# 168 keys of a block as 104 and 64 with the 64s of two heads transposed as one, v laid out by the host, key counts spread by a product, and a new order

## Chip, cores and metric

The kernel runs on one core of one Trainium2 chip. The metric is the device time of one execution in microseconds (us), a median over runs. The profile is of one execution; times inside it count from its first instruction.

## What is computed

Local attention with a few shared keys (4 batches, 8 heads of 64, 768 tokens), then a gated MLP with a product over the tokens:

```python
keep = (pos[None, :] < n_global) | ((rel >= 0) & (rel < n_local))      # 8 shared keys, 96 local ones
scores = where(keep, q @ k.T / 8 - slope[h] * dist, -1e9)
x = softmax(scores) @ v                                               # heads side by side: 4 x 768 x 512
h = relu(x @ w_in)                                                    # 512 -> 1024, halves u and v
v_s = einsum('ts,bsd->btd', w_spatial, layer_norm(v)) + b_spatial
out = (u * v_s) @ w_out                                               # 512 -> 512
```

## The kernel before

A block `n` is 128 queries of one batch (6 a batch, 24 in all; `i = n % 6`). A block with `i > 0` sees 168 keys: 64 queries need 8 shared and 96 local keys before their end, so each half of the block has its own 168. `prep` loads q and k. `scores` makes four score groups (16 small products on a quarter of the array each), then for each head one VectorE instruction (scale, bias, row minimum into `pr`) and one ScalarE exponential with its row sum. `values` transposes the probabilities on TensorE into PSUM tiles `p`, copies them to `pth` tiles, and multiplies them with `v`, two heads side by side in the array (64 columns each): the value product. Before, it cuts 168 keys into two chunks of 84 (`CK = KW // 2`): two transposes a head, 16 a block; a pair of heads fills one PSUM tile (84x512), so four copies a block (lines 830 to 839). Blocks with `i = 0` see 128 keys: 8 transposes and four copies of 128x256.

`prep_v` (line 742) loads v into one of two places of `vring`: for `i > 0` four pieces, of 84 and 76 rows for either half, and some of 8 rows for the shared keys; for `i = 0` one of 128 rows. All loads and stores are issued by SyncE's queue (SP), in order.

The MLP stages are called V (v half of `x @ w_in`, then the norm), U (u half), G (product with `w_spatial`), O (product with `w_out`). All inputs are float32, and the MLP weights are split into a high and a low float32r part by VectorE, ScalarE and GpSimd at the start (`split_weights`: tiles `u` and `wos` are loaded, `wc` is worked on, `w_in_h`, `w_in_l` and so on are the results; 8 tiles of w_in, of which V needs four and U the other four). The first batch's attention runs in the same stretch: below, the startup.

All instructions are recorded and then put in order by `plan` (line 339): a list scheduler over five engines, with a cost for each operation (`cost`) and a rank for each stage from the table `KEYS`; operations with several possible engines go where the plan starts them earliest. `keep_warm` (line 451) puts transposes of the identity (`s<-ident`, `m<-ident`, `p<-ident`: fillers, whose results nobody reads) into TensorE's long planned gaps.

The key counts `n_global` and `n_local` are loaded to all 128 partitions (lines 562, 563), made floats, and set the bias tiles, which the first softmax needs.

Of the kernel before, what the change touches and what calls it, by code (L numbers as in the profile page):

```python
# [26 lines left out]
CFG = {'vrelu': 'a', 'urelu': 'x', 'rs': 'p', 'bias0': 'xx', 'zero': 'pp', 'kept': 'pavp', 'bias1': 'vx', 'bias2': 'a', 'S': [['I01', 'A'], ['I00', 'T00', 'T01', 'A', 'V00', 'B00'], ['T02', 'T03', 'A', 'V01', 'U00'], ['T04', 'T05', 'A', 'V02'], ['Q00', 'Q01', 'A', 'V03', 'U01'], ['Q02', 'Q03', 'A', 'V04']], 'T': [['V15', 'U12', 'A'], ['G10', 'O10', 'A'], ['G11', 'O11', 'A'], ['G12', 'O12', 'V00', 'V01', 'U00', 'A'], ['V02', 'A'], ['V03', 'U01', 'A', 'V04']], 'END': ['V05', 'U02', 'G00', 'O00', 'G01', 'O01', 'G02', 'O02'], 'wcl': 'x', 'whi': 'x', 'wsub': 'x', 'wth': 'px', 'wtl': 'p', 'vhi': 'a', 'vlo': 'pp', 'qhi': 'x', 'qlo': 'x', 'khi': 'x', 'klo': 'x', 'pth0': 'aa', 'x0h': 'a', 'x0l': 'v', 'pth': 'x', 'xh': 'avva', 'c1': 'a', 'xl': 'pxxv', 'vnh': 'xapa', 'vnl': 'pvpv', 'gm': 'x', 'gh': 'aa', 'gl': 'x', 'o': 'vaaa', 'norm0': 'x', 'norm': 'x', 'vrn': 'v', 'fold': '0', 'div': 'x', 'rows': 'x', 'xf0h': 'x', 'xf0l': 'x', 'xbh': 'x', 'xbl': 'ppvv', 'b_rawqk': 1, 'b_ev': 3, 'b_raw': 1, 'b_pr': 10, 'b_pth': 5, 'b_c1': 2}  # L27
# [4 lines left out]
CK = KW // 2  # L32
# [184 lines left out]
def cost(op):  # L217
# [45 lines left out]
    return (180 if parts < P else 66) + (1.04 if parts < P else 1.1) * n, 0, not one  # L263


def shape_of(op):

    if op.eng != "tensor":
        return 0, 0
    if op.call != "together":  # L270
        return 0, 149 if op.call == "transpose" else 197
    return (1, 197) if list(op.args[0][2]["lhsT"].ap)[0][1] <= HALF else (2, 143)
# [66 lines left out]
def plan(ops, keys, trace=None):  # L339
# [18 lines left out]
    port, dma, mode = 0.0, 2500.0, 0  # L358
# [9 lines left out]
    while done < n:  # L368
# [115 lines left out]
WORDS = {"ev": 512, "gh": 1024, "gl": 1024, "pth": 512, "vring": 4096, "q": 512, "k": 960, "wos": 1024, "wts": 1536, "pr": 168, "s": 512, "p": 512, "m": 512, "c1": 512}  # L484
# [645 lines left out]
```

## Time and profile before

| | |
|---|---|
| median of 3 runs | 463.09 us (462.37 to 463.38) |
| the profiled execution | 462.34 us, its span 460.5 us |
| TensorE (PE) busy | 443.8 us, 96% of the span |
| VectorE (DVE), ScalarE (ACT), GpSimd (POOL) busy | 269.0, 196.6, 90.0 us |
| moved by DMA | 47.69 MB |

Busy times of PE are unions of overlapping matmuls, so the cost of one more matmul is read from the distance of starts or from the pieces of the chain of waits, not from its duration. A float32 product shows as two matmul records, a transpose as one.

### The profile page before, as it was taken

How to read it: one execution, taken by the hardware profiler on the slowest of the kernel's cores; microseconds unless marked ns; L12 is line 12 of the kernel's file. 1: busy time of each engine (PE TensorE's matmuls, PEld its weight loads, DVE VectorE, ACT ScalarE, POOL GpSimd, SP SyncE). 2: the span in 40 equal slices, each digit the busy share in tenths (PEclk: the TensorE clock that was granted, in tenths of full speed). 3: DMA queues.
4: the chain of work that ended last, by engine and by line, in shares of the span. 5: the costliest groups of instructions: out<-in, count | busy, mean ns of one | idle time of the engine just before them, and what ended most of it. 6: DMA issues, size and time to landing. Idle time of an engine off the chain costs nothing.

```text
span 460.5 us, 11598 instructions
## 1 busy us (share of the span) xinstructions
PE 443.8 (96%) x4621; PEld 398.5 (87%) x4621; DVE 269.0 (58%) x949; ACT 196.6 (43%) x594; POOL 90.0 (20%) x130
## 2 busy tenths in 40 slices
PE   6788999999999999999999999999999999999994
PEld 6577778899989989889989988989999888999994
DVE  5698988878883234686864334866632573324322
ACT  3558786657761121653762112666221362221111
POOL 2023456444120004221010003402100012330000
PEclk9899999999999999999999999999999999999998
DMA  6898775435641110334362110333111120000111
GB/s 187 254 308 254 222 249 159 124 125 168 203 142 74 47 47 0 111 97 125 106 210 95 47 46 1 127 124 98 41 47 47 45 60 1 1 2 2 46 47 53
DMA packets 23598, 47.69 MB, mean 104 GB/s; under 512 B 2704, under 2 KB 5008, under 8 KB 23536
## 3 DMA queue, kind: packets, MB, share of 16 engines
q1 hardware_dynamic: 23536, 46.87, 32.3%
q8 instruction: 38, 0.62, 0.6%
q14 instruction: 24, 0.20, 0.2%
HBM read 40.57 MB, written 6.29 MB: 102 GB/s over the span
## 4 chain that ended last, share of the span: by engine, by line
PE 86%; DVE 6%; DMA 3%; ACT 3%; issue 1%; SPq 0%; DVEq 0%
PE m L44 64%; PE p L44 17%; PE s L44 5%; DVE wc L44 2%; DMA u<-in_moe_w_in_dram 2%; DMA k<-in_k_dram 1%; ACT pr L44 1%; DVE pr L44 1%; DVE c L44 1%; DVE w_in_l L44 1%; SPq L44 0%; ACT w_in_h L44 0%; DVE pth L44 0%; ACT raw L44 0%; DVE xtl L44 0%
## 5 line engine op out<-in xcount | busy, mean ns | idle before, releaser
L44 ACT ACTIVATE pr<-pr,mn 128x168 f32<-128x168 f32 (+1 forms) x192 | 80.2, 419 | 18.7 <-DVE mn L44 16.5
L44 DVE CUSTOM_DVE_ANT_0 pr<-s,bias 128x168 f32<-128x168 f32 (+1 forms) x192 | 54.7, 316 | 22.7 <-PE p L44 15.9
L44 PE MATMUL p<-ident,pr 128*84 128x128 f32 (+1 forms) x352 | 54.6, 277 | 1.9 <-DVE c L44 0.6
L44 ACT ACTIVATE gh<-ev 128x512 fp32r<-128x512 f32 x24 | 15.1, 631 | 86.9 <-DVE ev L44 86.9
L44 DVE TENSOR_TENSOR ev<-m,b_bc 128x512 f32<-128x512 f32 x24 | 16.6, 690 | 60.7 <-PE m L44 60.6
L44 PEld LDWEIGHTS p<-pth,vring 84*64 84x64 f32 (+1 forms) x1344 | 43.2, 139 | 7.9 <-issue 3.3
L44 PE MATMUL p<-pth,vring 84*64 84x64 f32 (+1 forms) x1344 | 47.2, 228 | 2.7 <-ACT wc L44 2.6
L44 ACT ACTIVATE pth<-p 84x512 f32<-84x512 f32 (+1 forms) x65 | 35.8, 560 | 30.6 <-PE p L44 28.4
L44 ACT ACTIVATE ev<-m 128x512 f32<-128x512 f32 (+1 forms) x36 | 21.2, 590 | 64.4 <-PE m L44 64.4
L44 PEld LDWEIGHTS p<-ident,pr 128*84 128x84 f32 (+1 forms) x352 | 37.7, 122 | 11.0 <-ACT pr L44 1.9
L44 POOL TENSOR_TENSOR rs<-mv,eps 128x1 f32<-128x1 f32 x24 | 4.8, 201 | 197.6 <-DVE mv L44 123.3
L44 PE MATMUL m<-w_t_l,vnh 128*128 128x256 f32 x288 | 43.0, 283 | 0.0
L44 PE MATMUL m<-w_t_h,vnh 128*128 128x256 f32 x288 | 42.4, 282 | 0.0
L44 PE MATMUL m<-w_t_h,vnl 128*128 128x256 f32 x288 | 41.9, 281 | 0.0
L44 PEld LDWEIGHTS m<-w_t_h,vnh 128*128 128x128 f32 x288 | 37.9, 188 | 0.8
L44 PEld LDWEIGHTS m<-w_t_l,vnh 128*128 128x128 f32 x288 | 37.5, 188 | 0.0
L44 POOL TENSOR_TENSOR vnl<-ev,vnh 128x512 fp32r<-128x512 f32 x24 | 31.8, 1327 | 28.8 <-DVE vnh L44 21.5
L44 PEld LDWEIGHTS m<-w_t_h,vnl 128*128 128x128 f32 x288 | 37.2, 188 | 0.0
L44 ACT ACTIVATION_READ_ACCUMULATOR pr<-pr,mn 128x1 f32 x192 | 36.2, 188 | 0.0
L44 DVE TENSOR_SCALAR pr<-pr,rc 128x168 f32<-128x168 f32 (+1 forms) x125 | 35.7, 341 | 0.4
L44 PE MATMUL s<-k,q 64*64 64x168 f32 (+1 forms) x768 | 32.3, 303 | 1.7 <-DMA k<-in_k_dram 1.7
L44 DVE BATCH_NORM_STATS2 st<-ev 128x6 f32<-128x512 f32 x24 | 16.5, 690 | 27.6 <-ACT ev L44 27.5
(122 smaller groups left out, 810.0 us busy)
## 6 DMA issues: line engine op xcount, KB each, us to landing
k<-in_k_dram SPq DMA_DIRECT2D x20, 480.0 KB
vring<-in_v_dram SPq DMA_DIRECT2D x40, 168.0 KB
q<-in_q_dram SPq DMA_DIRECT2D x24, 256.0 KB
vring<-in_v_dram SPq DMA_DIRECT2D x40, 152.0 KB
out_dram<-ev SPq DMA_DIRECT2D x23, 256.0 KB
u<-in_moe_w_in_dram SPq DMA_DIRECT2D x8, 512.0 KB
wts<-in_moe_w_spatial_dram SPq DMA_DIRECT2D x6, 384.0 KB
wos<-in_moe_w_out_dram SPq DMA_DIRECT2D x8, 256.0 KB
```

The lines of the kernel that those rows point to most:

```text
L44: getattr(self.real, call)(*args, **kw)
```

## The change

The 168 keys are cut into 104 and 64. Each head's 104 are transposed alone (8 transposes a block); the 64 of the two heads of a pair lie side by side in one `pr` tile (`pair`, first head 104 then 64, second head 64 then 104) and are transposed as one 128x128 (4 a block). Four heads' 104s fill one PSUM tile, the four pairs' 64s another: three copies a block instead of four, and two of 128x512 instead of four of 128x256 for `i = 0`. The second value product of a head then runs over 128 rows, 64 of which meet zeros: the host lays v out so, and one load of 128 rows of 8 KB brings a block's whole v (1,048.6 KB instead of 655). The key counts are loaded to one partition, the other 127 set to zero, and a product with ones spreads them. The host's work is not in the time. The planner has other costs, other ranks (`KEYS`) and other numbers of buffers, so the order is new everywhere.

```diff
-... 'b_pr': 10, 'b_pth': 5, 'b_c1': 2}
+... 'b_pr': 6, 'b_pth': 4, 'b_c1': 2}
...
-CK = KW // 2
+REST = 64
+CK = KW - REST
...
-            return 2.5 + list(out.ap)[0][1] / 1.2, 0, False
+            return 2.5 + P / 1.2, 0, False
...
-        return 650, 2050 + n * 4 * parts * .0042, False
+        return 450, n * 4 * parts * .0026, False
...
-KEYS = {'start': -658.74, ('P', 0): -204.74, ...
+KEYS = {'start': -774.15, ('P', 0): -299.97, ...
...
     nraw = const.tile([P, 4], I32, name="nraw")
-    nc.sync.dma_start(out=nraw[:, 0:2], in_=n_global.bitcast(I32).partition_broadcast(P))
-    nc.sync.dma_start(out=nraw[:, 2:4], in_=n_local.bitcast(I32).partition_broadcast(P))
...
+    nc.vector.memset(nraw, 0)
+    nc.sync.dma_start(out=nraw[0:1, 0:2], in_=n_global.bitcast(I32).partition_broadcast(1))
+    nc.sync.dma_start(out=nraw[0:1, 2:4], in_=n_local.bitcast(I32).partition_broadcast(1))
...
+    nc.vector.memset(ones, 1.0)
+    nc.vector.tensor_copy(out=nf, in_=nraw)
...
+    nps = ps_p.tile([P, 2], F32, name="nps", tag="p")
+    nc.tensor.matmul(nps, lhsT=ones, rhs=nwide, start=True, stop=True)
+    nc.vector.tensor_copy(out=nwide, in_=nps)
...
     def prep_v(n):
         b, i = divmod(n, NB)
-        if n == 0:
-            ring["v"] = work.tile([P, 2, 2, 2, DM], F32, name="vt", tag="vring", bufs=1)
-        vt = ring["v"][:, n % 2]
...
-            nc.sync.dma_start(out=vt[0 if z else NGMAX:CK, 0, z], in_=v[b, end - (KW - NGMAX):cut, :])
-            nc.sync.dma_start(out=vt[0:end - cut, 1, z], in_=v[b, cut:end, :])
+        if i:
+            nc.sync.dma_start(out=vring[:, n % 2], in_=v[b, i, :, 0:4 * DM])
+        else:
+            nc.sync.dma_start(out=vring[:, n % 2, 0:DM], in_=v[b, i, :, 4 * DM:])
...
+            pair = work.tile([P, 2, W], F32, name="pr", bufs=nb("pr"))
+            probs.append(pair)
             for j in range(2):
                 h = 2 * g + j
-                pr = work.tile([P, W], F32, name="pr", bufs=nb("pr"))
-                probs.append(pr)
+                pr = pair[:, j]
...
+        def turned(k, parts):
+            pt = ps_p.tile([P, 4, P], F32, name="pt", tag="p")[0:k]
+            for x, part in enumerate(parts):
+                nc.tensor.transpose(pt[:, x], part, ident)
+            t = work.tile([P, 4, P], F32, name="pth", bufs=nb("pth"))[0:k]
+            cp(E("pth", len(pth)), t, pt)
+            pth.append(t)
+
+        for half in range(2):
+            if half:
                 yield
-            pt = ps_p.tile([P, nch, 2, P], F32, name="pt", tag="p")[0:K]
-            for j in range(2):
-                for c in range(nch):
-                    nc.tensor.transpose(pt[:, c, j], probs[2 * g + j][:, c * K:(c + 1) * K], ident)
-            t = work.tile([P, nch, 2, P], F32, name="pth", bufs=nb("pth"))[0:K]
-            cp(E("pth", g), t, pt)
-            pth.append(t)
+            turned(K, [probs[h // 2][:, h % 2, h % 2 * (W - K):][:, 0:K] for h in range(4 * half, 4 * half + 4)])
+        if i:
+            turned(P, [probs[g].rearrange("p a x -> p (a x)")[:, K:K + P] for g in range(NP)])
...
-                lhsT=vt[:, c, z, g * P + 64 * j:g * P + 64 * j + 64], rhs=pth[g][:, c, j, zs],
-                start=(c == 0), stop=(c == nch - 1),
+                lhsT=vr[:, z, j, g * 64:g * 64 + 64] if c else vt[0:K, z, g * P + 64 * j:g * P + 64 * j + 64],
+                rhs=pth[2][:, g, zs] if c else pth[g // 2][:, g % 2 * 2 + j, zs],
+                start=(c == 0), stop=(c == 1 or i == 0),
```

How the order moves, at three places. First TensorE in the second batch, one block with `i > 0` (products of other stages stand where rows are left out). Before:

```order
L44 MATMUL p_122<-ident,pr_99 84x128 x2
L44 MATMUL p_122<-ident,pr_100 84x128 x2
...
L44 MATMUL p_120<-ident,pr_101 84x128 x2
L44 MATMUL p_120<-ident,pr_102 84x128 x2
...
L44 MATMUL p_122<-ident,pr_105 84x128 x2
L44 MATMUL p_122<-ident,pr_106 84x128 x2
...
L44 MATMUL p_120<-ident,pr_107 84x128 x2
L44 MATMUL p_120<-ident,pr_108 84x128 x2
```

Of the change (`pr_122` and so on now hold two heads):

```order
L45 MATMUL p_118<-ident,pr_122 104x128 x2
L45 MATMUL p_118<-ident,pr_123 104x128 x2
...
L45 MATMUL p_118<-ident,pr_122 128x128
L45 MATMUL p_118<-ident,pr_123 128x128
L45 MATMUL p_118<-ident,pr_102 128x128
L45 MATMUL p_118<-ident,pr_103 128x128
...
L45 MATMUL p_87<-ident,pr_102 104x128 x2
L45 MATMUL p_87<-ident,pr_103 104x128 x2
```

A block's transposes went from 16 in four PSUM tiles to 12 in three. Over the whole program the order holds 376 transposes of data before and 296 now, and 105 fillers before and 63 now; the products of all other stages are as many as before. Second, SyncE's loads at the start of the program. Before:

```order
L44 DMA nraw<-in_n_global_dram 128x2
L44 DMA nraw<-in_n_local_dram 128x2
L44 DMA q_116<-in_q_dram 128x512
L44 DMA k_117<-in_k_dram 128x960
L44 DMA q_90<-in_q_dram 128x512
L44 DMA k_91<-in_k_dram 128x4x128
L44 DMA vring_110<-in_v_dram 8x512 x2
L44 DMA vring_110<-in_v_dram 76x512
L44 DMA vring_110<-in_v_dram 84x512 x2
L44 DMA vring_110<-in_v_dram 76x512
L44 DMA u_115<-in_moe_w_in_dram 128x1024
L44 DMA u_111<-in_moe_w_in_dram 128x1024
```

Of the change:

```order
L45 DMA q_93<-in_q_dram 128x512
L45 DMA nraw<-in_n_global_dram 1x2
L45 DMA nraw<-in_n_local_dram 1x2
L45 DMA k_94<-in_k_dram 128x4x128
L45 DMA q_114<-in_q_dram 128x512
L45 DMA k_115<-in_k_dram 128x960
L45 DMA b_bc<-in_moe_b_spatial_dram 128x768
L45 DMA u_109<-in_moe_w_in_dram 128x1024
L45 DMA wos_145<-in_moe_w_out_dram 128x512
L45 DMA u_111<-in_moe_w_in_dram 128x1024
L45 DMA wos_145<-in_moe_w_out_dram 128x512
L45 DMA u_113<-in_moe_w_in_dram 128x1024
```

The first v load now stands behind three tiles of w_in. Bytes issued up to and with the eighth tile of w_in, added up over these rows: 13.91 MB before, 16.74 MB now. Third, VectorE between the key counts and the first bias. Before:

```order
L44 CAST nf<-nraw 128x4
L44 SCALAR_TENSOR_TENSOR nwide<-nf 128x1 x2
L44 SCALAR_TENSOR_TENSOR nwide<-nwide,nf 128x1 x2
L44 TENSOR_SCALAR wide<-nwide 128x1 x3
L44 TENSOR_SCALAR ev_93<-ev_94,nwide 128x128
```

Of the change:

```order
L45 CAST nf<-nraw 128x4
L45 SCALAR_TENSOR_TENSOR nwide<-nf 128x1 x2
L45 SCALAR_TENSOR_TENSOR nwide<-nwide,nf 128x1 x2
L45 COPY nwide<-p_87 128x2
L45 TENSOR_SCALAR ev_96<-ev_97,nwide 128x128
```

The copy waits for the product with ones, which is TensorE's first instruction now, ahead of all score products; 33 fillers stood there before. Up to the last instruction that writes w_in_h or w_in_l, VectorE has 228 instructions before and 203 now.

## Rows read from the trace of the kernel before

**Rows 1.** Windows, whole core: us, busy of each engine, clock, DMA share, GB/s.
```profile
0.00:80.00 80.00, 69.34 (x889) 57.35 (x893) 66.33 (x246) 52.49 (x168) 28.90 (x37) 0.98 0.78 234
80.00:155.00 75.00, 75.00 (x873) 68.43 (x866) 52.84 (x220) 40.60 (x133) 20.00 (x31) 1.00 0.42 136
...
380.00:455.00 75.00, 74.47 (x616) 68.86 (x614) 25.77 (x44) 14.42 (x25) 11.14 (x16) 1.00 0.05 17
```
**Rows 2.** Windows of TensorE alone, after the startup.
```profile
80.00:454.00 374.00, 374.00 (x3738) 1.00 0.24 76
```
**Rows 3.** Groups by form, TensorE's fillers: count, busy us, mean ns, idle before.
```profile
L44 PE MATMUL s<-ident 128*128 128x128 f32 x64 | 9.9, 319 | 1.7 <-POOL ident masks.py:199 1.7
...
L44 PE MATMUL m<-ident 128*128 128x128 f32 x36 | 4.9, 279 | 0.0
...
L44 PE MATMUL p<-ident 128*128 128x128 f32 x5 | 0.8, 284 | 0.0
```
**Rows 4.** Chain of waits in order of time, TensorE in the steady part: start us, us, what.
```profile
204.22 0.44 PE p L44 x4
...
207.21 1.30 PE s L44 x32
208.51 2.02 PE p L44 x64
...
214.97 0.87 PE p L44 x8
...
219.44 2.02 PE p L44 x64
...
229.44 2.58 PE p L44 x68
...
293.85 0.22 PE p L44 x2
...
297.47 1.02 PE p L44 x16
```
**Rows 5.** Groups by form, transposes of data and the weights of value products.
```profile
L44 PE MATMUL p<-ident,pr 128*84 128x128 f32 x320 | 48.3, 277 | 0.9 <-DVE c L44 0.6 <-ACT pth L44 0.2
...
L44 PEld LDWEIGHTS p<-pth,vring 84*64 84x64 f32 x1280 | 39.0, 138 | 4.4 <-issue 3.1 <-ACT pth L44 0.7 <-DMA vring<-in_v_dram 0.2
...
L44 PEld LDWEIGHTS p<-pth,vring 128*64 128x64 f32 x64 | 4.2, 158 | 3.6 <-ACT wc L44 2.8 <-ACT pr L44 0.4 <-issue 0.2
```
**Rows 6.** Groups by form, copies of transposed probabilities out of PSUM.
```profile
L44 ACT ACTIVATE pth<-p 84x512 f32<-84x512 f32 x55 | 32.1, 593 | 29.7 <-PE p L44 27.6 <-DVE ev L44 1.6
...
L44 DVE COPY pth<-p 84x512 f32<-84x512 f32 x25 | 16.9, 681 | 4.8 <-PE p L44 4.5
...
L44 ACT ACTIVATE pth<-p 128x256 f32<-128x256 f32 x10 | 3.7, 380 | 0.9 <-PE p L44 0.8
```
**Rows 7.** Windows of the startup, whole core, columns as in rows 1.
```profile
5.00:10.00 5.00, 3.27 (x44) 3.06 (x47) 4.19 (x25) 1.00 (x5) 0.78 (x3) 1.00 1.01 337
25.00:30.00 5.00, 4.54 (x82) 3.83 (x81) 4.77 (x10) 1.80 (x4) 1.46 (x2) 1.00 1.02 348
...
35.00:65.00 30.00, 28.04 (x389) 21.93 (x382) 26.84 (x95) 25.31 (x79) 14.50 (x13) 1.00 0.77 234
...
0.00:71.60 71.60, 61.44 (x821) 50.43 (x822) 59.32 (x230) 47.76 (x154) 22.19 (x30) 0.98 0.81 243
```
**Rows 8.** Waits of SyncE's queue: total us, times, longest us.
```profile
SPq L44 <- DMA vring<-in_v_dram: 21.3, 21, 2.3
```
**Rows 9.** Timeline of the startup, ACT, PE and DVE: start us, us, [idle before <-releaser].
```profile
62.31 0.67 ACT L44 ACTIVATE wc<-u 128x512 f32<-128x512 f32 x1
...
63.84 0.67 ACT L44 ACTIVATE wc<-u 128x512 f32<-128x512 f32 x1
...
69.67 0.62 PE L44 MATMUL m<-xth,w_in_h 128*128 128x256 f32 x3
...
70.93 0.69 DVE L44 TENSOR_TENSOR w_in_l<-wc,w_in_h 128x512 fp32r<-128x512 f32 x1
```
**Rows 10.** Timeline of the first 20 us, DVE, PE and ACT.
```profile
5.63 0.17 DVE L44 CAST nf<-nraw 128x4 f32<-128x4 int32 x1 [3.28 <-DMA nraw<-in_n_local_dram]
...
9.31 1.10 PE L44 MATMUL s<-k,q 64*64 64x128 f32 x32 [1.73 <-DMA k<-in_k_dram]
...
19.22 0.66 ACT L44 ACTIVATE wc<-u 128x512 f32<-128x512 f32 x1 [2.37 <-DMA u<-in_moe_w_in_dram]
```

More of the change, by code (lines that the diff above doesn't have):

```diff
@@ L262, in cost @@
         return 145, 0, False
-    return (180 if parts < P else 66) + (1.04 if parts < P else 1.1) * n, 0, not one
+    return 66 + 1.07 * n, 0, not one
 def shape_of(op):
@@ L270, in shape_of @@
     if op.call != "together":
[L271 to L272 removed]
+        return 0, 149 if op.call == "transpose" else 190
+    return (1, 135) if list(op.args[0][2]["lhsT"].ap)[0][1] <= HALF else (2, 150)
 def lengths(op):
@@ L279, in lengths @@
     tiles = 4 if shape_of(op)[0] == 1 else 2
-    return [4 * elements(kw["rhs"]) * .422 / tiles for _, _, kw in op.args]
+    return [4 * elements(kw["rhs"]) * .417 / tiles + (2 if tiles == 4 else 5) for _, _, kw in op.args]
 def link(ops):
@@ L357, in plan @@
     free = dict.fromkeys(names, 0.0)
-    port, dma, mode = 0.0, 2500.0, 0
+    port, dma, mode = 0.0, 0.0, 0
     wait = {x: [] for x in names}
@@ L433, in plan @@
         if e == "sync":
-            dma = max(dma, t + 1200) + (op.late - 2050)
-            stand = dma + 1400
+            dma = max(dma, t + 1400) + op.late
+            stand = dma + 600
         done += 1
@@ L481, in keep_warm @@
     return out
-WORDS = {"ev": 512, "gh": 1024, "gl": 1024, "pth": 512, "vring": 4096, "q": 512, "k": 960, "wos": 1024, "wts": 1536, "pr": 168, "s": 512, "p": 512, "m": 512, "c1": 512}
+WORDS = {"ev": 512, "gh": 1024, "gl": 1024, "pth": 512, "vring": 4096, "q": 512, "k": 960, "wos": 1024, "wts": 1536, "s": 512, "p": 512, "m": 512, "c1": 512, "pr": 2 * KW}
 BUFS = {"gh": 1, "gl": 1, "u": 3, "s": 4, "p": 2, "m": 2, "wc": 2, "wos": 1, "wts": 1}
@@ L592, in attn_then_spatial_gating_kernel @@
     bias0 = pers.tile([P, H, P], BF16, name="bias0")
+    ones = work.tile([P, P], F32, name="ones", tag="c1", bufs=nb("c1"))
+    nc.vector.memset(ones, 1.0)
+    nc.vector.tensor_copy(out=nf, in_=nraw)
+    for j in range(2):
+        low, high, n = nf[:, 2 * j:2 * j + 1], nf[:, 2 * j + 1:2 * j + 2], nwide[:, j:j + 1]
+        nc.vector.scalar_tensor_tensor(out=n, in0=low, scalar=0.0, in1=high, op0=ALU.is_lt, op1=ALU.add)
+        nc.vector.scalar_tensor_tensor(out=n, in0=n, scalar=float(2 ** 32), in1=low, op0=ALU.mult, op1=ALU.add)
+    nps = ps_p.tile([P, 2], F32, name="nps", tag="p")
+    nc.tensor.matmul(nps, lhsT=ones, rhs=nwide, start=True, stop=True)
+    nc.vector.tensor_copy(out=nwide, in_=nps)
     eps = const.tile([P, 1], F32, name="eps")
@@ L731, in attn_then_spatial_gating_kernel @@
     ring = {}
+    halves = [slice(64 * j, 64 * j + 64) for j in range(2)]
     def prep(n):
@@ L740, in prep, with pieces @@
         return qt, kt
+    vring = work.tile([P, 2, 4 * DM], F32, name="vt", tag="vring", bufs=1)
+    def pieces(n):
+        vt = vring[:, n % 2]
+        return vt[:, 0:2 * DM].rearrange("p (z m) -> p z m", z=2), vt[:, 2 * DM:].rearrange("p (z j m) -> p z j m", z=2, j=2)
     def prep_v(n):
         b, i = divmod(n, NB)
-        if n == 0:
-            ring["v"] = work.tile([P, 2, 2, 2, DM], F32, name="vt", tag="vring", bufs=1)
-        vt = ring["v"][:, n % 2]
-        if i == 0:
-            nc.sync.dma_start(out=vt[:, 0, 0], in_=v[b, 0:P, :])
-            return
-        if i == 1:
-            nc.sync.dma_start(out=vt[0:NGMAX, 0, 0], in_=v[b, 0:NGMAX, :])
-        if i <= 2:
-            nc.sync.dma_start(out=vt[CK - NGMAX:CK, 1, 1], in_=v[b, 0:NGMAX, :])
-        for z in range(2):
-            end = i * P + HALF * (z + 1)
-            cut = end - (KW - NGMAX) + CK - (0 if z else NGMAX)
-            nc.sync.dma_start(out=vt[0 if z else NGMAX:CK, 0, z], in_=v[b, end - (KW - NGMAX):cut, :])
-            nc.sync.dma_start(out=vt[0:end - cut, 1, z], in_=v[b, cut:end, :])
+        if i:
+            nc.sync.dma_start(out=vring[:, n % 2], in_=v[b, i, :, 0:4 * DM])
+        else:
+            nc.sync.dma_start(out=vring[:, n % 2, 0:DM], in_=v[b, i, :, 4 * DM:])
     xt = {}
-    halves = [slice(64 * j, 64 * j + 64) for j in range(2)]
     held = {}
@@ L821, in values @@
         b, i = divmod(n, NB)
-        nch, K = (2, CK) if i else (1, P)
-        vt = ring["v"][0:K, n % 2]
+        W, K = (KW, CK) if i else (P, P)
+        vt, vr = pieces(n)
         if i % 2 == 0:
@@ L848, in values @@
             ("matmul", (ops[s_, g, zs],), dict(
-                lhsT=vt[:, c, z, g * P + 64 * j:g * P + 64 * j + 64], rhs=pth[g][:, c, j, zs],
-                start=(c == 0), stop=(c == nch - 1),
+                lhsT=vr[:, z, j, g * 64:g * 64 + 64] if c else vt[0:K, z, g * P + 64 * j:g * P + 64 * j + 64],
+                rhs=pth[2][:, g, zs] if c else pth[g // 2][:, g % 2 * 2 + j, zs],
+                start=(c == 0), stop=(c == 1 or i == 0),
             ))
-            for g in range(NP) for z, zs in enumerate(halves if i else [slice(0, P)]) for c in range(nch) for j, s_ in enumerate(halves)
+            for g in range(NP) for z, zs in enumerate(halves if i else [slice(0, P)]) for c in range(2 if i else 1) for j, s_ in enumerate(halves)
         ])
@@ L1109, with rows @@
         elif name == "v":
-            a = a.transpose(0, 2, 1, 3).reshape(a.shape[0], a.shape[2], -1)
+            a = a.transpose(0, 2, 1, 3)
+            at = _np.arange(0, a.shape[1], P)[:, None]
+            shared = _np.broadcast_to(_np.arange(NGMAX), (len(at), NGMAX))
+            lower, upper = (at + _np.arange(x - KW + NGMAX, x) for x in (HALF, P))
+            keys = [_np.maximum(_np.concatenate(x, axis=1), 0) for x in ((shared, lower), (upper, shared))]
+            def rows(x, j, n):
+                x = _np.concatenate([x, x[:, :n]], axis=1)[:, :n]
+                return a[:, x, j::2].reshape(a.shape[0], len(at), n, -1, 1, a.shape[3])
+            first = [_np.concatenate([rows(x[:, :CK], 0, P), rows(x[:, REST:], 1, P)], axis=4).reshape(a.shape[0], len(at), P, -1) for x in keys]
+            rest = [_np.stack([rows(x[:, CK:], 0, REST), rows(x[:, :REST], 1, REST)], axis=2).reshape(a.shape[0], len(at), 2, REST, -1) for x in keys]
+            rest = [_np.stack([_np.pad(x[:, :, j], ((0, 0), (0, 0), (j * REST, P - REST - j * REST), (0, 0))) for j in range(2)], axis=3) for x in rest]
+            rest = [x.reshape(a.shape[0], len(at), P, -1) for x in rest]
+            a = _np.concatenate(first + rest + [a.reshape(a.shape[0], len(at), P, -1)], axis=3)
         elif name == "moe_w_spatial":
```

21 lines of the change are left out of this document (7 added, 14 removed).

## Prediction

> **What bounds the kernel now.** I read three views. The windows come first: from 80 us on PE is busy in all of its time, 374.00 of 374 us [rows 2], while DVE needs 52.84 of the next 75 us, falls to a third by the end, and the DMA engines go from 0.42 busy to 0.05 [rows 1]. So after 80 us the time is TensorE's work alone: a product less there is its time less, and a copy or a load less is worth nothing. Before 80 us it is otherwise: PE is idle for 10.7 us, and 105 of its instructions, 15.6 us busy, are fillers [rows 1, 3]. Some 26 us of the startup do no work. There DVE is busy for 66.33 of 80 us, and the DMA engines for 0.78 of it. Groups and chain pieces give prices; the startup's timeline tells what PE waits for.
>
> **The transposes.** A piece of four lasts 0.44 us and one of eight 0.87 [rows 4], so one costs 109 ns; their durations (277 ns [rows 5]) overlap. 20 blocks with four fewer make 80 fewer: 80 x 0.109 = **-8.7 us**. The new ones take 104 or 128 columns where 84 were. Those of blocks with `i = 0` have 128 today, and two of them last 0.22 us, 110 ns each (at 293.85 us) [rows 4]; 104 lies between two equal prices. So no change for the other 240, and the term is firm; their changed place in the order belongs to the last term.
>
> **The value products.** Their number stays, 64 records a block, and so do their moving columns, 64 each. The rows rise from 84 to 104 and 128. A block costs 2.02 us, or 31.5 ns a record, with 84 rows and 64 columns; blocks with `i = 0` have 128 rows and 128 columns and cost 1.02 us for 16 records, 64 ns, just twice [rows 4]. So 128 rows cost no more than 84 for each column, and I take **0**. Against it: the weight loads of 128 rows last 158 ns on average, those of 84 rows 138 [rows 5]; 20 ns on 1280 records, if it were all paid, is +25.6 us, which is the upper bound and a rival below.
>
> **The copies.** 20 of 593 to 681 ns disappear for `i > 0`, and 16 of 256 columns become 8 of 512 [rows 6]. After 80 us nothing waits for them. What hides them is PE's own queue of MLP products; if it ran dry, each block's last copy would show, 0.6 us. Off the end: 0 there; in the startup five copies less, 3 us shared by ACT and DVE.
>
> **The v loads.** Four to six issues a block become one of 1,049 KB. At 337 to 348 GB/s [rows 7] that is 3.1 us, against 10.9 us from one value product to the next (starts at 208.51 and 219.44) [rows 4]; its place in `vring` comes free a whole block ahead. Hidden after 80 us: 0. If three blocks were planned 6 us apart, with some 2 us of waiting each, that cover would be thin: up to +3 us.
>
> **The key counts.** The float copy waits for them until 5.63 us, and the first scores for k until 9.31 [rows 10]. Two loads of 128 rows of 8 bytes shrink to one row each and one q load goes ahead. Added are two fills, one product and one copy on DVE, whose result the first bias waits for, with all DVE work queued behind; nearest rows are a 0.17 us DVE instruction [rows 10] and a filler's 0.28 us [rows 3], with two passes from engine to engine some 0.8 us. Saved: between 0 and the 3.28 us wait. PE's first instruction now waits for these counts with every score product behind it, but k was the later one before. I take -1, inside the next term.
>
> **The startup, where the rest is decided.** What PE lacks there is MLP work: stage U starts at 69.67 us, while the eighth w_in tile is first read at 63.84 and its last part written at 70.93 [rows 9]. Two things bound that moment.
> Loads: up to the eighth tile 13.91 MB were issued, and 16.74 MB now. In the windows in which mostly loads of 128 rows are under way (q and k; k, w_out, biases, w_spatial) the engines move 337 and 348 GB/s at a share of 1.0; from 35 to 65 us, with v pieces of 76 and 84 rows between, it is 234 at 0.77, and SP, the issuing queue, waits 21 times for v pieces, 21.3 us in all [rows 7, 8]. At 234 the eighth tile would land at about 4 + 71.5 = 75 us, 12 later than now; at 340 at 4 + 49 = 53 us, 10 earlier. All large loads now have 128 rows, so the nearer row is 340.
> The Trainium skill, page "DMA: Bandwidth & Descriptors", section on why a DMA increments its semaphore by 16, has a rule: a load runs on the largest number of engines, up to 16, that divides its rows, so 76 rows on 4, 84 on 14, 128 on 16. By it four engines carry every piece; up to the eighth tile I count 1,118 KB on each of them before and 1,046 on each of 16 now. That agrees with a share of 0.77 beside a waiting queue (no view here shows single engines), and as an estimate from the page it says less than the rows: at the old pace of one engine 306 GB/s, the tile at 59 us, and a sum of 452.
> VectorE: up to 71.6 us it was busy 59.32 [rows 7]. Of its 228 instructions up to there 25 are gone, eight of them copies of 0.68 us, in all some 9 us by the mean durations: 50 us of work, and with the same 12 us of idle time 62.
> Both give U about 8 us earlier. The order puts some 2.6 us less useful product work ahead of U (37.9 to 35.3, counted at the prices above), which then has to be done later. So the startup gives **-5.5 us**; bounds -12 (all of the load bound, and DVE filled) and +3 (DVE as before, less work ahead of U). Fewer fillers (63) are no gain of their own, only its sign.
>
> **The new order afterwards.** PE waits for nothing there now, so it can only lose: **+0.5**, up to +4, where blocks stand closer together. The changes between score products, value products and the rest are 82 before and 83 now, at 0.13 us (a piece of 68 against one of 64 and four transposes [rows 4]): nothing.
>
> Sum on the profiled execution: 462.34 - 8.7 - 5.5 + 0.5 = 448.6 us. It lies 0.75 us under the median of the runs shown, so 449.4; I say **449**.
>
> **Rivals.**
> *The startup stays* (0.17): DVE and ACT carry it, whatever lands earlier. For: DVE busy 66.33 of 80 us. Against: its 13.7 us of idle time and the 25 instructions less. 463.1 - 8.7 = 454, to 456 with some later idling.
> *The loads gain a part* (0.15): 300 GB/s, between 234 and 348. 4 + 55.8 = 60 us for the eighth tile, 4 earlier than its read at 63.84, and -1.4 after the 2.6 us: 453.
> *The startup falls by the whole load bound* (0.17): 463.1 - 8.7 - 12 = 442.
> *Rows cost in the value products* (0.04), the slower end: place, each of 1280 records; price, up to 20 ns; 463.1 - 8.7 - 5.5 + 25.6 = 474.5. It decides from 11 ns on (14.2 / 1280). For it, the weight loads' 158 against 138; against it, the exact double in blocks with `i = 0`.
> *The bytes decide* (0.04): the rate stays at 234 GB/s. U then starts 12 us later; 463.1 - 8.7 + 9 = 463.4, no change that can be measured.
> That the transposes do not go is excluded by the order: 376 became 296.
>
> **Numbers.** The forecast (446 to 452) has 0.43. The range, 441 to 456.5, takes in the first three rivals: 0.92, about 0.82 after what their tails lose. 0.2% of the time, 0.9 us, is what a measurement here can tell. The last two give same 0.03 and slower 0.05; faster 0.92.
>
> **What would show it.** Transposes: 160 of 104 and 112 of 128 columns, pieces of four still 0.44 us. Value products: pieces of 64 still 2.02 us; 2.4 or more is the rows' rival. Startup: U at about 62 us, DMA share near 1.0 at over 300 GB/s up to 45 us, waits of SP for v pieces gone, PE full from about 72 us. If U starts at 69 or later while DVE is full, the startup stays; if DVE waits for `wc` and the DMA share is full at 240 GB/s, the bytes decide. After the startup a PE idle time over 4 us would make the order the fault.

## The result

| | before | after |
|---|---|---|
| median | 462.95 us (462.37 to 463.38, 4 runs) | 445.2 us (444.8 to 446.27, 4 runs) |
| the profiled execution, its span | 462.34 us, 460.5 us | 444.82 us, 443.0 us |

The ratio is 0.9621, 95% interval 0.9599 to 0.9643: 17.75 us less.

### The profile page after: what moved, and what is told of

Read it like the earlier page. It is cut to its first block, busy times and chain, and to the rows that moved or that the text cites. A ratio compares the mean times of both kernels' runs of the same rounds, so it can differ in the third digit from the quotient of the medians.

```text
span 443.0 us, 11193 instructions
## 1 busy us (share of the span) xinstructions
PE 428.3 (97%) x4501; PEld 386.2 (87%) x4501; DVE 261.9 (59%) x918; ACT 193.9 (44%) x585; POOL 99.4 (22%) x145
## 4 chain that ended last, share of the span: by engine, by line
PE 91%; DMA 4%; ACT 2%; SPq 1%; issue 0%; DVE 0%; ACTq 0%
PE m L45 68%; PE p L45 17%; PE s L45 6%; DMA vring<-in_v_dram 2%; DMA u<-in_moe_w_in_dram 2%; ACT pr L45 1%; SPq L45 1%; ACT pth L45 1%; DVE pr L45 0%; ACT raw L45 0%; ACT ev L45 0%; ACT wc L45 0%; ACT c L45 0%; DVE mn L45 0%; ACTq L45 0%
## 5 line engine op out<-in xcount | busy, mean ns | idle before, releaser
L45 ACT ACTIVATE pr<-pr,mn 128x168 f32<-128x168 f32 (+1 forms) x192 | 79.9, 419 | 10.7 <-DVE mn L45 10.7
L45 DVE CUSTOM_DVE_ANT_0 pr<-s,bias 128x168 f32<-128x168 f32 (+1 forms) x192 | 51.7, 319 | 17.4 <-PE p L45 11.9
L45 ACT ACTIVATE ev<-m 128x512 f32<-128x512 f32 (+1 forms) x36 | 21.3, 591 | 74.3 <-PE m L45 66.8
L45 PEld LDWEIGHTS p<-pth,vring 128*64 128x64 f32 (+1 forms) x1344 | 42.4, 137 | 6.4 <-issue 1.2
L45 PE MATMUL p<-ident,pr 128*104 128x128 f32 (+1 forms) x272 | 44.9, 277 | 3.0 <-ACT pr L45 1.7
L45 PE MATMUL p<-pth,vring 128*64 128x64 f32 (+2 forms) x1344 | 46.1, 225 | 1.3 <-DMA vring<-in_v_dram 0.9
L45 PE MATMUL m<-w_t_h,vnl 128*128 128x256 f32 x288 | 43.7, 284 | 0.0
L45 PE MATMUL m<-w_t_h,vnh 128*128 128x256 f32 x288 | 43.5, 284 | 0.0
L45 ACT ACTIVATE pth<-p 104x512 f32<-104x512 f32 (+1 forms) x54 | 31.6, 594 | 21.9 <-PE p L45 21.3
L45 PEld LDWEIGHTS p<-ident,pr 128*104 128x104 f32 (+1 forms) x272 | 30.9, 134 | 10.7 <-ACT pr L45 2.8
L45 PEld LDWEIGHTS m<-w_t_h,vnl 128*128 128x128 f32 x288 | 38.1, 189 | 0.0
```

Source lines behind the costliest of these rows:

```text
L45: getattr(self.real, call)(*args, **kw)
```

## The profile after

Windows of the changed kernel, whole core, columns as in [rows 1], and TensorE alone after the startup:

```profile
0.00:80.00 80.00, 71.08 (x918) 60.12 (x920) 72.87 (x284) 58.81 (x188) 36.39 (x47) 1.00 0.76 279
...
80.00:437.00 357.00, 357.00 (x3587) 1.00 0.26 91
```

After 80 us PE is full as before [rows 2]. Ahead of it DVE does 72.87 us of work where it did 66.33, and PE ends 29 records more, although fillers went from 105 to 63. Fillers by form, to set beside [rows 3]:

```profile
L45 PE MATMUL m<-ident 128*128 128x128 f32 x49 | 6.2, 272 | 0.0
...
L45 PE MATMUL p<-ident 128*128 128x128 f32 x14 | 2.7, 369 | 0.0
```

PE's idle time and fillers in the first 80 us are 8.9 + 8.9 = 17.8 us, where they were 10.7 + 15.6 = 26.3: 8.5 us more of useful work. Then the transposes, the weights of the value products, and the chain in the steady part, to set beside [rows 4, 5]:

```profile
L45 PE MATMUL p<-ident,pr 128*104 128x128 f32 x160 | 26.4, 276 | 0.3 <-ACT c L45 0.3
...
L45 PE MATMUL p<-ident,pr 128*128 128x128 f32 x112 | 20.7, 279 | 2.7 <-ACT pr L45 1.7 <-DVE pth L45 0.5 <-ACT pth L45 0.2
...
L45 PEld LDWEIGHTS p<-pth,vring 128*64 128x64 f32 x704 | 35.9, 137 | 2.0 <-DMA vring<-in_v_dram 1.1 <-issue 0.4 <-DMA wos<-in_moe_w_out_dram 0.4
L45 PEld LDWEIGHTS p<-pth,vring 104*64 104x64 f32 x640 | 32.3, 137 | 4.4 <-ACT pth L45 1.1 <-issue 0.9 <-ACT pr L45 0.7
```

```profile
195.86 0.44 PE p L45 x4
...
196.53 0.44 PE p L45 x4
...
198.11 2.02 PE p L45 x64
200.13 1.30 PE s L45 x32
```

Four transposes still cost 0.44 us, those of 128 columns (at 195.86) and those of 104 (at 196.53), a block's value products 2.02 us; 104 and 128 rows load their weights in 137 ns, as 84 rows did. The startup, again by windows, beside [rows 7]:

```profile
5.00:10.00 5.00, 4.87 (x54) 4.40 (x58) 4.91 (x35) 2.90 (x14) 1.39 (x4) 1.00 0.89 257
10.00:15.00 5.00, 3.25 (x46) 2.15 (x37) 3.90 (x20) 2.84 (x11) 0.57 (x2) 1.00 1.03 394
...
25.00:30.00 5.00, 4.53 (x88) 3.56 (x90) 5.00 (x24) 5.00 (x20) 4.58 (x4) 1.00 1.02 411
...
50.00:55.00 5.00, 5.00 (x88) 4.29 (x85) 5.00 (x8) 4.73 (x16) 2.17 (x1) 1.00 0.77 262
```

```profile
52.78 0.68 ACT L45 ACTIVATE wc<-u 128x512 f32<-128x512 f32 x1
```

From 10 to 40 us the loads run at 394 to 411 GB/s, not at the 340 that the forecast took. The second fence is a row of ACT's timeline: the eighth tile of w_in is read at 52.78 us (63.84 before [rows 9]). The waits of SP for `vring` fell from 21.3 us [rows 8] to 2.2.

## The experiments

For every kernel the table gives the median, the start of the last `wc<-u` on DVE (DVE's last work with the eighth tile of w_in; the trace by tile), and the mean rate from 10 to 45 us (windows). Before was timed again beside each group of kernels, at 462.49 to 463.19 us; the changed kernel was not, so a few tenths of a us between it and the kernels made from it mean nothing.

| kernel | us | last `wc<-u`, us | GB/s |
|---|---|---|---|
| before | 462.95 | 68.1 | 273 |
| after | 445.2 | 57.0 | 402 |
| a_twice | 453.57 | 58.0 | 400 |
| a_bcast | 449.23 | 61.1 | 372 |
| a_first | 444.94 | 58.1 | 401 |
| a_rows76 | 497.42 | 87.7 | 259 |
| a_rows64 | 469.88 | 78.4 | 295 |
| a_cols | 444.98 | 57.1 | 399 |
| a_evenodd | 444.9 | 57.7 | 397 |
| b_spread | 459.89 | 66.0 | 261 |
| b_fastv | 460.33 | 65.2 | 366 |
| b_onev | 472.65 | 77.0 | 327 |
| a_oldplan | 468.93 | 77.2 | 353 |
| a_84 | 469.88 | 60.4 | 396 |

Names that begin with a start from the changed kernel, those with b from the kernel before.

### The transposes: a_twice

```diff
         for op in keep_warm(plan(nc.ops, KEYS), spare, filler):
             op.issue()
+            if op.call == "transpose" and getattr(op, "again", False):   # the shared pieces
+                op.issue()
```

> The changed kernel, order kept, with each transpose of a shared piece issued twice in a row, so that a block again issues 16 transposes (80 more in all, the same result). Theory A (TensorE is full after the startup, a transpose is worth its 0.109 us): 20 blocks of which 15 or 16 lie after the startup, so 64 of the 80 count in full and the rest in part: +7.0 to +8.7 us, 452.2 to 454 us. Rival F (transposes hide beside waits): +3 us or less.

Measured 453.57 us (ratio to before 0.9809, 0.9794 to 0.9825): +8.4 us for 80 transposes, 105 ns each. The forecast's 109 ns and its 8.7 us hold.

### The key counts: a_bcast and a_first

```diff
-    nc.sync.dma_start(out=nraw[0:1, 0:2], in_=n_global.bitcast(I32).partition_broadcast(1))
+    nc.sync.dma_start(out=nraw[:, 0:2], in_=n_global.bitcast(I32).partition_broadcast(P))
...
-    nc.vector.memset(ones, 1.0)
+    nc.vector.memset(ones, 1.0 / P)
```

> The changed kernel, order kept, with the key counts loaded into all 128 partitions again (two loads of 128 x 2 in place of 1 x 2); the product stays, with ones of 1/128, so only the loads differ. Theory A: nf casts at 5.5 us or later in place of 3.40, the first scores some 2 us later, of which the startup hands on 0 to 2 us: 445 to 447.5 us. Rival C (the early counts made a large part of the startup's gain): 449 us or more.

Measured 449.23 us (0.9723, 0.9704 to 0.9742): **+4.0 us**, a miss for theory A's "0 to 2 us"; rival C had 449 or more. DVE's timeline, of the changed kernel and of a_bcast:

```profile
3.40 0.17 DVE L45 CAST nf<-nraw 128x4 f32<-128x4 int32 x1 [1.04 <-DMA nraw<-in_n_local_dram]
```

```profile
5.70 0.17 DVE L45 CAST nf<-nraw 128x4 f32<-128x4 int32 x1 [3.34 <-DMA nraw<-in_n_local_dram]
```

2.3 us at the front became 4.1 at the last `wc<-u` (57.0 to 61.1). The traces show the way. At its `wc<-u,wc` of 22.45 us DVE is only 1.1 us late (21.35 in the changed kernel). Then this instruction and the next, 0.68 us each in the changed kernel, last 1.27 and 2.31 us, and GpSimd is at work beside them. DVE of the changed kernel, then DVE and GpSimd of a_bcast:

```profile
21.95 0.68 DVE L45 TENSOR_TENSOR w_in_l<-wc,w_in_h 128x512 fp32r<-128x512 f32 x1
```

```profile
22.45 1.27 DVE L45 SCALAR_TENSOR_TENSOR wc<-u,wc 128x512 int32<-128x512 int32 x1
23.64 2.31 DVE L45 TENSOR_TENSOR w_in_l<-wc,w_in_h 128x512 fp32r<-128x512 f32 x1
```

```profile
22.34 0.83 POOL L45 TENSOR_SCALAR w_t_h<-wts 128x768 fp32r<-128x768 f32 x1 [9.38 <-DMA wts<-in_moe_w_spatial_dram]
23.26 2.14 POOL L45 TENSOR_TENSOR w_t_l<-wts,w_t_h 128x768 fp32r<-128x768 f32 x1
```

In the changed kernel this GpSimd work starts at 22.73 us, when both DVE instructions are over. So DVE's next result (`c`) is 3.0 us late, PE waits 1.97 us for it and then 1.04 for `pth`, and the granted clock falls, as a_bcast's windows show:

```profile
25.00:30.00 5.00, 2.35 (x11) 1.80 (x12) 5.00 (x23) 3.21 (x14) 3.76 (x4) 0.85 1.02 407
30.00:35.00 5.00, 5.00 (x104) 4.26 (x103) 3.89 (x16) 4.55 (x16) 0.29 (x1) 0.81 0.89 326
```

It is 0.85 and 0.81 where the changed kernel has 1.00. Behind these waits PE is 2.9 us late (28.30 for 25.43), and its next four groups of matmuls take 4.37 us (28.30 to 32.67) in place of 3.21 (25.43 to 28.64), which makes it 4.0. So of the 4.0 us some 1.1 are the late start itself, 1.8 the two long DVE instructions and 1.2 the clock. That GpSimd's work is what stretched DVE's wasn't tried apart; the two only coincide.

The other way, the counts ahead of everything on SP's queue, worked out in one partition:

```diff
-    nc.vector.memset(nraw, 0)
...
-    nc.tensor.matmul(nps, lhsT=ones, rhs=nwide, start=True, stop=True)
+    nc.tensor.matmul(nps, lhsT=ones[0:1], rhs=nwide[0:1], start=True, stop=True)
...
+        for op in first + [op for op in planned if op not in first + left]:   # first: the two count loads
```

> The changed kernel, order kept, with the two loads of the key counts ahead of the first load of q on SP's queue: the clearing of nraw goes, and the counts are worked out and spread from one partition alone (ones of 1 x 128). The loads' issue moves from 1.17 to some 0.72 us, so nf should cast 0.4 to 0.7 us sooner, at 2.7 to 3.0 us. If each us of the counts is worth what the broadcast loads showed (4.0 us for 2.3 us), 444.0 to 444.5 us against 445.2; theory K (the first scores wait for k by then, 0.47 us at 5.13, so that earlier counts find nothing to start): 445.2 us, within 0.5 us.

Measured 444.94 us (0.961, 0.9589 to 0.963): no change against 445.2, as theory K has it. PE's timelines, of the changed kernel and of a_first, show why:

```profile
4.08 0.59 PE L45 MATMUL p<-nwide,c 128*128 128x2 f32 x2 [4.08 <-DVE nwide L45]
5.13 1.99 PE L45 MATMUL s<-k,q 64*64 64x128 f32 x32 [0.47 <-DMA k<-in_k_dram]
```

```profile
3.03 0.58 PE L45 MATMUL p<-nwide,c 1*128 1x2 f32 x2 [3.03 <-DVE nwide L45]
5.26 1.99 PE L45 MATMUL s<-k,q 64*64 64x128 f32 x32 [1.65 <-DMA k<-in_k_dram]
```

The counts are there 1.05 us sooner (4.08 to 3.03), and the scores wait for k instead, 1.65 us. The counts are worth their time only down to where k lands.

### The rows of a v load under the new order: a_rows76, a_rows64, a_cols, a_evenodd

All four keep the order of every engine and the bytes; one load of 128 rows x 2048 becomes two. The cuts are `slice(0, 76)` and `slice(76, P)` (a_rows76), `slice(0, 64)` and `slice(64, P)` (a_rows64), even and odd rows (a_evenodd), and the two halves of the columns (a_cols):

```diff
-            nc.sync.dma_start(out=vring[:, n % 2], in_=v[b, i, :, 0:4 * DM])
+            nc.together(nc.sync, [("dma_start", (), dict(out=vring[x, n % 2], in_=v[b, i, x, 0:4 * DM])) for x in (slice(0, 64), slice(64, P))])
```

> The changed kernel with its one load of v a block cut by rows into 76 and 52; bytes, order and all other work stay. Theory A (row counts that few DMA engines share slow all loads behind them): the waits of SP for v come back, 20 to 30 us moves 360 GB/s or less, U ends its wait later, and the time rises by 4 to 12 us, to 449 to 457 us. Rival B (the order made the gain): 445 us, within 1 us.

> The control to the cut at 76 rows: the changed kernel with its one load of v a block cut into 64 and 64 rows, so twice the issues but rows that spread evenly. Theory A and rival B alike: 445 us, within 0.7 us. A theory E, that the number of loads counts and not their rows: as slow as the cut at 76 rows.

> The changed kernel with its one load of v a block cut by columns into two loads of 128 rows x 1024: as many loads as the cut at 64 rows, half as long rows, but each load over all 128 partitions. Theory P (a load is fast only if it spreads over all partitions): 445 us, within 1.5 us, and some 400 GB/s in the startup. Theory E (the number of loads costs): as slow as the cut at 64 rows, 466 to 472 us.

> The changed kernel with its one load of v a block cut into even rows and odd rows: 64 rows a load as in the control that came out at 469.88 us, but each spread over all 128 partitions. Theory P (the stretch of partitions that a load covers sets its rate): 445 us, within 1.5 us. Theory R (64 rows are too few, wherever they lie): 466 to 472 us.

Measured: a_rows76 497.42 us (1.0757, 1.0694 to 1.082), a_rows64 469.88 (1.0127, 1.0093 to 1.0161), a_cols 444.98 (0.9614, 0.9572 to 0.9656), a_evenodd 444.9 (0.9604, 0.9554 to 0.9653). Theory A's 449 to 457 for a_rows76 was far too low. The control at 64 and 64 rows, which both theories had at 445, came out some 24 us above it (its ten runs lie between 463.7 and 471.0 us), and led to the other two. They settle it: 64 rows are as good as 128 if they lie in every second partition, and slow if they lie side by side. Two issues in place of one cost nothing. Windows of a_rows64, then of a_evenodd:

```profile
15.00:20.00 5.00, 4.07 (x36) 3.60 (x34) 3.74 (x15) 3.97 (x16) 0.00 (x0) 1.00 1.02 210
20.00:25.00 5.00, 1.74 (x14) 1.50 (x14) 4.02 (x9) 2.77 (x8) 0.00 (x0) 1.00 1.01 269
25.00:30.00 5.00, 3.64 (x40) 3.11 (x44) 0.98 (x4) 0.84 (x1) 2.54 (x2) 0.50 1.04 407
...
35.00:40.00 5.00, 4.55 (x87) 4.14 (x84) 4.93 (x19) 4.35 (x14) 1.17 (x2) 1.00 1.02 222
```

```profile
15.00:20.00 5.00, 4.57 (x41) 4.10 (x40) 4.41 (x15) 4.66 (x17) 0.00 (x0) 1.00 1.02 404
...
35.00:40.00 5.00, 5.00 (x108) 4.36 (x107) 4.55 (x17) 4.11 (x17) 4.75 (x4) 1.00 1.01 393
```

Both show the DMA engines busy (share 1.01 and more), and yet 210 and 222 GB/s against 404 and 393: a full share says that transfers are under way, not how fast. The Trainium skill, page "SBUF — State Buffer", section "Door 1: The DMA port swizzle (why `[64,N]` ≈ `[32,N]`)", says that the rate goes by how many of 16 ports the partitions reach, and that 64 partitions side by side reach 8; by its table of ports, every second one of 128 reaches all 16. The traces agree: about half the rate in the one, all of it in the other.

The loss is larger than the late loads. In a_rows64 PE waits 4.00 us for `vring` ahead of 26.36 us, the granted clock of the window around it is 0.50 (1.2 GHz), and the pieces that follow run slowly: 16 value products last 1.97 us, 1.09 in the changed kernel. PE's timelines, of a_rows64 and of the changed kernel:

```profile
26.36 1.97 PE L45 MATMUL p<-pth,vring 128*64 128x128 f32 x16 [4.00 <-DMA vring<-in_v_dram]
```

```profile
21.72 1.09 PE L45 MATMUL p<-pth,vring 128*64 128x128 f32 x16 [0.87 <-DMA vring<-in_v_dram]
```

a_rows76 adds 27.5 us to a_rows64. PE's waits in the two, a_rows64 first:

```profile
PE p L45 <- DMA vring<-in_v_dram: 6.3, 3, 4.0
```

```profile
PE p L45 <- DMA vring<-in_v_dram: 26.0, 8, 9.4
```

Whether the row counts as such or the longer of two halves makes the difference wasn't tried apart. One window of a_rows76 speaks for the row counts:

```profile
25.00:30.00 5.00, 0.00 (x0) 0.00 (x0) 0.00 (x0) 0.00 (x0) 0.00 (x0) 0.50 0.61 197
```

PE, DVE, ACT and GpSimd stand still there, and the share is 0.61, where a_rows64 has 1.04 in the same window. So part of the DMA engines' time is idle while the kernel waits for v, and the Trainium skill's rule of rows and engines that the prediction weighed stays open for loads of 76 rows.

### The v loads under the old order: b_spread, b_fastv, b_onev

b_spread issues each piece as two loads (76 rows as 64 and 12, 84 as 80 and 4), planned as one:

```diff
-            nc.sync.dma_start(out=vt[0:end - cut, 1, z], in_=v[b, cut:end, :])
+            spread(vt[0:end - cut, 1, z], v[b, cut:end, :])   # rows // 16 * 16, and the rest
```

> The kernel before with every load of v cut in two on the same queue (76 rows as 64 and 12, 84 as 80 and 4); order, transposes, copies and products stay as they are. Theory A (the startup's gain of some 9 us comes from loads of v that keep all 16 DMA engines at work): 20 to 30 us moves near 400 GB/s in place of 348, the last wc<-u ends by 57 us in place of 64, and the time falls to 452 to 458 us. Rival B (the gain comes from the new order and costs alone): 462 to 464 us, with the moved GB/s unchanged or its gain unused.

Measured 459.89 us (0.9938, 0.992 to 0.9957): -2.6 us, less than the 4.5 to 10.5 that theory A had, and the rate did not rise at all (261 GB/s against 273). So the number of engines that share a load's rows, the rule that the prediction weighed from the Trainium skill (page "DMA: Bandwidth & Descriptors", section on why a DMA increments its semaphore by 16), isn't what held the rate here, or not alone; the pieces still lay in partitions 0 to 83. Where the 2.6 us come from stays open.

b_fastv records the old pieces, so that the old order comes out, and issues one load of 128 host-laid rows in place of a block's pieces:

```diff
+        planned = list(keep_warm(plan(nc.ops, KEYS), spare, filler))
...
+            elif x in at:
+                op.real.dma_start(**op.big[1])
```

> The kernel before with its order kept on every engine, only that the loads of one block's v are replaced, at the place of the first of them (of the last, in a batch's third block), by one load of 128 host-laid rows. Theory A (under this order the loads of v were what held the startup): 450 to 457 us, the last wc<-u by 57 us in place of 64. Rival B (under the old order the other engines, not the loads, set the startup's end, so that the faster loads need a new order): 459 to 463 us. A fall to 472 us, as where the old table replanned around one load, would mean that the single load itself hurts.

Measured 460.33 us (0.9953, 0.994 to 0.9967): rival B. The loads now run at 366 GB/s and yield 2.3 us. What SyncE's queue waits for longest in the first 52 us has changed, from v to DVE's work on w_in, which frees the three buffers of `u` (before, then b_fastv):

```profile
SPq L44 <- DMA vring<-in_v_dram: 12.8, 13, 2.3
```

```profile
SPq L44 <- DVE wc L44: 13.5, 5, 3.9
```

ACT's and SP's timelines of b_fastv, the eighth tile's load (the later of the two) and its reading:

```profile
43.03 1.66 SPq L44 DMA_DIRECT2D u<-in_moe_w_in_dram  x2
```

```profile
60.91 0.67 ACT L44 ACTIVATE wc<-u 128x512 f32<-128x512 f32 x1
```

It is issued some 16 us before ACT reads it, and the w_in loads of this kernel land after 6.6 us (median) and 11.2 at most. So what stands ahead of it on ACT and DVE in the order, not the load, sets the moment.

b_onev plans one load a block with the old table and old costs (the load of a_84, below, put into the kernel before):

```diff
+            nc.sync.dma_start(out=ring["v"][:, n % 2].rearrange("p c z m -> p (c z m)"), in_=v[b, i, :, 0:4 * DM])
```

> The kernel before with one part of the change alone: v host-laid and loaded in one go of 128 rows a block (chunks of 84 and 84 as they were; 44 rows of each load are never read), all else, order tables and costs too, as before. Theory A (the single load makes the startup's gain): no wait of SP for v, 15 to 45 us near 400 GB/s, the last wc<-u by 57 us, and 451 to 456 us. Rival B (an order made for the slow loads can't use fast ones; only the replanning did): 459 us or more, although the loads move as fast.

Measured 472.65 us (1.0199, 1.0153 to 1.0244), **slower than before** and in rival B's range, with 386 to 416 GB/s from 5 to 25 us. Given one load in place of four, the old table makes another order, in which the last `wc<-u` starts at 77.0 us (68.1 before).

### The order: a_oldplan and a_84

```diff
-KEYS = {'start': -774.15, ('P', 0): -299.97, ...
+KEYS = {'start': -658.74, ('P', 0): -204.74, ...
```

a_oldplan has the table and all planner costs of before.

> The changed kernel with the planner's table and costs of the kernel before, so replanned by the old rules. Theory A (the order adds little): 445 to 450 us, with loads near 400 GB/s from 15 to 40 us. Rival B (each order fits only the kernel that it was searched for, as 84 and 84 under the new table, 469.88 us, suggests): 455 to 470 us, lost as idle TensorE in many places after the startup.

Measured 468.93 us (1.0129, 1.0086 to 1.0172): rival B for the size (+24 us), but the loss is in the startup. Its eighth tile is issued at 50.15 us and read only here (SP's and ACT's timelines):

```profile
50.15 0.33 SPq L45 DMA_DIRECT2D u<-in_moe_w_in_dram  x1
```

```profile
72.50 0.68 ACT L45 ACTIVATE wc<-u 128x512 f32<-128x512 f32 x1
```

PE spends the time on fillers, 243 in place of 63, the longest group of them:

```profile
L45 PE MATMUL s<-ident 128*128 128x128 f32 x128 | 16.1, 277 | 0.0
```

a_84 goes back to 84 and 84 keys and 16 transposes, with the one load, the counts and the new table:

```diff
-REST = 64
-CK = KW - REST
+CK = KW // 2
...
+                turned(K, [probs[h // 2][:, h % 2, c * K:(c + 1) * K] for h, c in heads])
```

> The changed kernel with keys cut as 84 and 84 again (16 transposes of 128 columns a block in place of 12, copies 84x512 four a block in place of three), v host-laid and loaded in one go of 128 rows a block, the key counts by the product. Theory A (the transposes are worth their time on TensorE, 80 times 0.109 us, the startup keeps its gain): 452 to 455 us. Rival D (fewer copies and shared pieces give more than the transposes' own time): 456 us or more. A rival F (the transposes are hidden by other waits): 447 us or less.

Measured 469.88 us (1.0151, 1.0129 to 1.0173), +24.7 us where the transposes explain 8.4. That is rival D's range, but not its reason shown: the table was searched for the other cut. Its last `wc<-u` is 3.4 us late, and PE has new holes long after the startup, for instance fillers at 139.82 and here (PE's timeline):

```profile
145.11 3.00 PE L44 MATMUL s<-ident 128*128 128x128 f32 x26
```

With 4.0 us of such fillers and 2.9 us of waits after 80 us, some 6 us of its loss stay open. What 84 and 84 would give with a table of their own wasn't tried. Neither was one that searched for a better table; no kernel here beats the changed one by more than the measurement tells.

## Why the prediction was right, step by step

The forecast of 449 was 3.8 us too high, inside its range; "faster" was right. Its steps:

- **The bound.** Right: PE is full from 80 us on before and after, and most kernels lost or gained in the startup; a_twice (more work on PE), a_84 and a_rows76 (PE 69.90 of the 80 us after it) also lost later.
- **The transposes, -8.7.** Right: 160 and 112 as said, 0.44 us for four, and -8.4 by a_twice.
- **Value products and copies, 0.** Right: 2.02 us, weights 137 ns. The rival in which rows cost has fallen.
- **v loads after the startup, 0.** Right: no wait of PE lies after 80 us.
- **The key counts, -1.** This is the step whose size was off most: 4.0 by a_bcast. It was priced as a wait of 3.28 us at most that k would cover. k does cover what comes earlier still (a_first). But the 2.3 us of a_bcast grew to 4.1 at the last `wc<-u`, by two long DVE instructions and a lower clock of PE, and the sum had no term for such growth.
- **The startup, -5.5.** Measured some 9.35 (17.75 less 8.4), of which 4.0 are the counts. Three numbers in it were off. The loads were taken at 340 GB/s from windows that still held narrow loads, and moved 402; the bound by the Trainium skill's count of engines (page "DMA: Bandwidth & Descriptors"; an estimate of 306 GB/s, a sum of 452) was further off. DVE's work, put at 50 us, is 54.18 up to 60 us, and its idle time, kept at 12 us, is 60 - 54.18 = 5.8; these two errors partly cancel:

```profile
0.00:60.00 60.00, 51.08 (x757) 42.48 (x758) 54.18 (x210) 45.39 (x145) 25.29 (x29) 1.00 0.91 333
```

U's run of products starts at 57.86 us, where 62 was foretold and 69.67 was before.
- **Its reason, that faster loads bring U forward.** Half right. Slow loads do cost under the new order (some 24 us for a_rows64), but fast loads alone give only 2.3 us under the old one (b_fastv). The eighth tile is read long after it is issued in all of these kernels: I took its reading for its landing. Beyond the transposes and the counts 17.75 - 8.4 - 4.0 = 5.3 us are left, which loads and order make together; that the three parts add up wasn't tried.
- **The new order, +0.5.** Right as far as it went, after the startup: PE is busy for 357.00 of 357 us. But it counted the order as a risk only. The old table on the new kernel costs 24 us, so the replanning is a part without which the rest came out slower than before. That the sum landed within 4 us of the result owes something to luck here: nothing in it told a table that fits from one that doesn't.

## What to carry to other kernels

In these runs a load's rate went by the partitions that it covers: lay data out so that one load covers all 128, or at least spreads over them; the busy share doesn't show the loss, the GB/s of a window do. Where a searched order holds a kernel together, an edit to one part must be tried with the order kept (issue differently, plan the same) and again with the order searched anew; replanning by a table that was searched for another kernel mixed the edit's worth with a misfit of 12 to 24 us (b_onev against b_fastv, a_84, a_oldplan). And a small thing that the fullest engine of a startup waits for first can be worth more than its own wait, by what the delay runs into (2.3 us became 4.0 in a_bcast), or nothing once something else comes later (a_first).

## What the hardware showed that was not expected

- Two loads of 64 rows of 8 KB, side by side, run at some 210 to 222 GB/s; even and odd rows at 393 to 404, at the same DMA share of 1.01 to 1.02.
- This one core moved up to 411 GB/s (25 to 30 us).
- The cast that waits for the key counts starts 2.3 us later with two broadcast loads of 128 x 2 numbers than with two of 1 x 2 (5.70 against 3.40 us).
- Two DVE instructions of 0.68 us lasted 1.27 and 2.31 us in a_bcast, in a stretch in which GpSimd worked on `w_t_h` and `w_t_l`.
- A wait of 4.00 us of PE in the startup went with a granted clock of 0.50 (1.2 GHz) in that window and with pieces of nearly twice their length behind it (1.97 us for 1.09).
